# A fused adaLN spectral and MLP layer, forward and backward: sums of x, small rows, index tables, one modulation row and two w1 loads stand elsewhere in the order

## The chip, the core and the metric

The kernel runs on one core of a Trainium2 chip. The metric is the device time of one execution in microseconds (us). The profile is of one execution. Its span runs from the first to the last instruction, and the execution's own time is a little longer than that.

## What is computed

Forward, with x of 2048 tokens by 1024 features:

```python
mod = silu(c) @ w_mod                      # six rows of 1024: sa, ca, ga, sb, cb, gb
h = layernorm(x) * (1 + ca) + sa
x = x + ga * irfft2(rfft2(h) * (w_r + 1j * w_i))
h = layernorm(x) * (1 + cb) + sb
y = layernorm(h); z = y @ w1 + b1          # 1024 -> 3584
out = x + gb * (gelu(z) @ w2 + b2)
```

Given grad_out, the kernel returns the output and the gradients with respect to x, w_r, w_i, w1, b1, w2, b2, c and w_mod. All of it is in bf16 with sums in fp32.

## The kernel before

The work runs as one program of five engines with queues of their own: TensorE (PE) multiplies, VectorE (DVE) and ScalarE (ACT) copy, scale and sum, GpSimd (POOL) makes index tables and issues gathers and stores, SyncE (SP) issues most loads. A scheduler places each engine's instructions; `tc.issue_after(x)` and `ordered()` hold an instruction behind another in that order, `tc.high_priority()` prefers it. Each queue is worked in order: an instruction that waits holds those behind it.

SBUF is cut into regions named by tags (px0 to px5, uv0 to uv3, ph, fr, sma and so on). A new tile on a tag waits until all users of the tile before it are done.

The program's first stage, on which the change bears, has these parts:

- **Modulation rows.** `mod_block(r, h)` (L273 to L284) multiplies half a row of w_mod, a 1 MB block `wblk` that SP loads (L271) into px3, px4 or px5 in turn. Rows: 5 is gb, 1 is ca, 0 is sa, 2, 3 and 4 are ga, sb and cb.
- **Turns of grad_out.** `turn_go(j, cch)` (L541 to L554) turns block j of 512 tokens of grad_out (`go`) with 32 small matmuls into `gBoT[j]`; even pieces are copied out of PSUM by DVE (L550), odd ones by ACT (L553). Block j + 1 is turned between the matmuls of block j.
- **ph = gBoT times w2^T.** For each of 28 pieces fc of the hidden features, `ph_part` (L533) makes four PSUM tiles `pp` of 8 matmuls each. `ph_out` (L523) copies each into a slot `phs[fc % 4]` (three in `pho`, the fourth, `phr`, on tag ph) and POOL stores the slot to `d_ph` when its four tiles are there. The weights `wt` are w2^T in four slots, each loaded by a transposing DMA on SP (`load_w2t`, L342) four pieces ahead. Pieces 0 and 1 are done inside the turns; pieces 2 to 10 (`PH_EARLY` = 10) stand before the spectral part, the rest among its steps and behind it.
- **Sums of x.** x lies in four tiles `x4s[i]`, half of whose rows come by SP and the other half by gathers of POOL. `ln_act` (L455) takes the mean and variance of tile 1 on ACT, with eight passes over 128x1024; `ln_dve` (L470) those of tiles 0, 2 and 3 on DVE; `norm_act` (L496) normalises on ACT.
- **Index tables.** The sine and cosine matrices come from tables of integers: POOL multiplies (L378), DVE masks (L405), ACT takes the sine (L410). `gidx` on tag px0 holds two tables; so the third waits until ACT has read the first. Six tables of 128x1024 make the token matrices `smA` and `smB`, four of 128x512 make `em`.
- **Folds.** L927 to L938: DVE multiplies the normalised tiles in `fbuf` by 1 + ca and folds them along tokens and features, and adds the folded row of sa (`saf`). The spectral part's first matmuls (`pu`, L613) read the folded tiles. They stand in PE's queue behind piece 10 of ph.
- **Small rows.** `small_rows` (L900) makes grad b2's row by one small matmul (`ptr`, L210), stores it from `gb2r` to out_7, and turns b1 into a column (L205). The space for these rows is the end of `genv`, the scratch of the index tables on tag px2. The spectral part's weights `ws2` come next on px2, partly by SP and partly by gathers of POOL (L633).

The spectral part then alternates matmuls with DVE's complex products over eight pairs. `consume_fwd` (L943) works through its four results while PE does the rest of ph. After that come the MLP forward (`z_block` L1036, `bo_pass` L1089), with w1 in seven tiles of 1 MB loaded on SP by `load_w1` (L977), and the backward products. `load_w1` is called in the loop over fc (L991) with one tile at fc = 24, one at 25 and five at 27; the first two lie on px2 and px0.

## Time and profile before

| what | us |
|---|---|
| three runs | 1400.81, 1403.65, 1410.85 |
| the profiled execution, its own time | 1399.52 |
| its span | 1397.7 |
| PE busy in the span | 1360.1 |
| PE idle in the first 140.5 us | 26.2 |
| PE idle from there to 400 us | 6.9 |
| DVE busy in the span | 1069.4 |

Read from the windows by stage: PE is busy 97% of the span. It does the same matmuls whatever their order, so the time goes where PE waits, and where its clock is low behind a wait. In a row of the timeline, the first number is the start, the second the time from the start of the first to the end of the last of the instructions that the row merges, and the bracket gives the engine's idle time before it and what ended that.

### The profile page before, as it was taken

Reading aid. Unit: us, or ns where it says so; the run is one execution under the profiler, and the core shown is the slowest. Engines: PE = TensorE matmul, PEld = TensorE weight load, DVE = VectorE, ACT = ScalarE, POOL = GpSimd, SP = SyncE. Lnnn points to the kernel's source line nnn. Section 1 sums busy time; section 2 is a strip of 40 time slices with the busy share of each in tenths; the row PEclk is TensorE's granted clock in tenths of the full one; section 3 lists DMA queues with packets and bytes.
Section 4 is the critical chain, followed back from the end, with each engine's and each line's share of the span. In section 5 each row is a group of like instructions: output and inputs, shape, how many; then the busy total and the mean of one; then the engine's idle time right before and its main releaser. Section 6 shows DMA issues by size and latency. Waiting matters only on the chain.

```text
span 1397.7 us, 18662 instructions
## 1 busy us (share of the span) xinstructions
PE 1360.1 (97%) x6931; PEld 655.8 (47%) x6931; DVE 1069.4 (77%) x1479; ACT 763.4 (55%) x1082; POOL 380.0 (27%) x438
## 2 busy tenths in 40 slices
PE   6898999998999999999999999999999999999999
PEld 3343657443344444444444444444555555454444
DVE  5787698998899787787721297889987678968990
ACT  4762756675887765665602765436633364544311
POOL 4266271220212122122121010111444320332341
PEclk9999999999999999999999999999999999999999
DMA  9964474799888687597899869988679969899991
GB/s 325 296 192 121 128 181 144 219 268 350 239 252 270 220 268 256 176 281 241 235 324 252 202 197 247 330 264 220 209 237 265 239 143 250 216 246 251 293 333 66
DMA packets 356177, 330.08 MB, mean 236 GB/s; under 512 B 203834, under 2 KB 298448, under 8 KB 355958
## 3 DMA queue, kind: packets, MB, share of 16 engines
q1 hardware_dynamic: 313990, 200.76, 55.6%
q0 software_dynamic: 35328, 120.26, 25.2%
q10 hardware_dynamic: 6768, 7.87, 1.7%
q8 instruction: 54, 0.88, 0.3%
q14 instruction: 37, 0.30, 0.1%
HBM read 165.73 MB, written 114.87 MB: 201 GB/s over the span
## 4 chain that ended last, share of the span: by engine, by line
PE 74%; DVE 4%; ACT 3%; DMA 2%; issue 1%; DVEq 0%; ACTq 0%
PE pg L1205 14%; PE gw2acc L1377 14%; PE gw1acc L1641 14%; PE pbo L1105 11%; PE pz L1051 9%; PE pp L537 6%; DVE gt L195 2%; PE po L845 2%; DMA wt<-in_B_w_dram 1%; PE pcs L652 1%; PE pu L1521 1%; DMA w2sA<-in_B_w_dram 1%; ACT gt L1062 1%; ACT gt L1054 1%; ACT gt L1064 1%
## 5 line engine op out<-in xcount | busy, mean ns | idle before, releaser
L537 PE MATMUL pp<-gBoT,wt 128*128 128x512 bf16 x832 | 190.2, 386 | 9.7 <-ACT pho L529 4.8
L1205 PE MATMUL pg<-w1T,gzr 128*128 128x512 bf16 x896 | 196.0, 379 | 0.0
L1641 PE MATMUL gw1acc<-gzh,n3n 128*128 128x512 bf16 x640 | 139.6, 379 | 0.0
L1051 PEld LDWEIGHTS <-w 128*128 128x128 bf16 x896 | 87.7, 98 | 110.3 <-issue 7.2
L1205 PEld LDWEIGHTS <-gzr 128*128 128x128 bf16 x896 | 86.6, 98 | 108.6 <-issue 6.1
L1641 PEld LDWEIGHTS <-n3n 128*128 128x128 bf16 x896 | 87.4, 98 | 105.2 <-issue 1.3
L537 PEld LDWEIGHTS <-wt 128*128 128x128 bf16 x832 | 82.3, 99 | 108.2 <-issue 14.6
L1051 PE MATMUL pz<-n3Ta,w 128*128 128x512 bf16 x448 | 100.5, 384 | 2.6 <-ACT gt L1054 2.6
L1051 PE MATMUL pz<-n3Tb,w 128*128 128x512 bf16 x448 | 99.2, 379 | 0.2 <-DVE w2sD L1127 0.2
L195 DVE TENSOR_TENSOR ct<-ct 128x2048 bf16<-128x2048 bf16 (+1 forms) x84 | 91.4, 1116 | 2.3 <-ACT ct L1334 1.4
L1105 PEld LDWEIGHTS <-hhA 128*128 128x128 bf16 x608 | 58.9, 98 | 72.6 <-issue 2.3
L1645 ACT CAST gwo<-gw1acc 128x512 bf16<-128x512 f32 x56 | 32.4, 583 | 110.4 <-PE gw1acc L1641 93.5
L1054 ACT ACTIVATE gt<-pz,b_col 128x512 bf16<-128x512 f32 x112 | 72.2, 684 | 37.2 <-PE pz L1051 37.0
L1377 PE MATMUL gw2acc<-gB,hhsA 128*128 128x512 bf16 x416 | 92.4, 379 | 0.0
L1062 ACT ACTIVATE gt<-gt 128x2048 bf16<-128x2048 bf16 x28 | 53.5, 1911 | 56.3 <-DVE gt L195 56.3
L195 DVE TENSOR_TENSOR gt<-gt,gt 128x2048 bf16<-128x2048 bf16 x56 | 68.3, 1223 | 14.7 <-ACT gt L1064 13.5
L1385 ACT CAST gwo<-gw2acc 128x512 bf16<-128x512 f32 x40 | 23.6, 589 | 87.4 <-PE gw2acc L1377 70.2
L1377 PEld LDWEIGHTS <-hhsA 128*128 128x128 bf16 x416 | 40.8, 98 | 47.1
L529 ACT CAST pho<-pp 128x512 bf16<-128x512 f32 x55 | 31.1, 585 | 49.3 <-PE pp L537 39.3
L1058 ACT ACTIVATE gt<-gt 128x2048 bf16<-128x2048 bf16 x28 | 53.4, 1907 | 5.1 <-DVE w2sA L195 2.3
L1641 PE MATMUL gw1acc<-gzu,n3n 128*128 128x512 bf16 x256 | 55.4, 379 | 0.0
L1064 ACT ACTIVATE gt<-gt 128x2048 bf16<-128x2048 bf16 x28 | 53.4, 1909 | 0.5
(385 smaller groups left out, 2593.9 us busy)
## 6 DMA issues: line engine op xcount, KB each, us to landing
gzr<-d_gz SPq DMA_DIRECT2D x28, 512.0 KB
wblk<-in_w_mod_dram SPq DMA_DIRECT2D x12, 1024.0 KB
d_ph<-pho POOLq DMA_DIRECT2D x21, 512.0 KB
out_dram<-otl POOLq DMA_DIRECT2D x40, 256.0 KB
d_hh<-hhA POOLq DMA_DIRECT2D x19, 512.0 KB
wrw<-in_w_mod_dram SPq DMA_DIRECT2D x32, 256.0 KB
out_dram<-gwo POOLq DMA_DIRECT2D x57, 128.0 KB
w<-in_B_w_dram SPq DMA_DIRECT2D x7, 1024.0 KB
```

Of the source, the lines that this page charges most:

```text
L195: return nc.vector.tensor_tensor(out=out, in0=a, in1=b, op=op)
L537: last_pe[0] = nc.tensor.matmul(pp[:], lhsT=wt[:, fc % 4, cch, :], rhs=gBoT[j][:, cch, :], start=(cch == 0), stop=(cch == NDC - 1))
L1051: last_pe[0] = nc.tensor.matmul(pz[:], lhsT=w1s[g][:, cch, k * P:(k + 1) * P], rhs=n3T[:, cch, :], start=(cch == 0), stop=(cch == NDC - 1))
L1054: z_in = nc.scalar.activation(out=zb[:, k, :], in_=pz[:], func=ACT.Identity, bias=b1_col[:, fc:fc + 1], scale=1.0)
L1058: nc.scalar.activation(out=av, in_=zb, func=ACT.Square)
L1062: nc.scalar.activation(out=sg, in_=bv, func=ACT.Sigmoid, scale=2.0 * GK)
L1064: nc.scalar.activation(out=bv, in_=bv, func=ACT.Sigmoid, scale=-2.0 * GK)
L1105: last_pe[0] = nc.tensor.matmul(pbs[i][:], lhsT=hh[:, k, i * P:(i + 1) * P], rhs=wp[:, k, :], start=False, stop=(g == 6 and k == 3))
L1205: last_pg[0] = nc.tensor.matmul(pgs[i][:], lhsT=gzs[b, g][:, k, i * P:(i + 1) * P], rhs=w1Ts[g][:, k, h * KH:(h + 1) * KH], start=(g == 0 ...
L1377: nc.tensor.matmul(acc[:], lhsT=hh_of(fc)[:, t, :], rhs=gBs[t // 4][:, t % 4, h * KH:(h + 1) * KH], start=(t == 0), stop=(t == NT - 1))
L1641: nc.tensor.matmul(acc[:], lhsT=n3ns[t // 4][:, t % 4, cch * P:(cch + 1) * P], rhs=gz2[t // 8][:, t % 8, :], start=(t == 0), stop=(t == NT ...
L1645: w1g["ev"] = nc.scalar.copy(out=ob, in_=acc[:])
```

## The change

- The small rows (c, grad b2, b1) lie in a tile `phx` on tag ph, beside the reversing matrix `irev`, no longer in `genv`. `small_rows` is called at fc = 2, not 4, and the fourth slot `phr` (also on tag ph) is opened behind it.
- The sums of x tiles 0 and 1, and their norms, are ordered behind the last copies of grad_out's second turn (`turn_in`), no longer ahead of the turns.
- Two more index tables, `gidx2` on tag px1 (where grad_out's block 0 lay), make four; tables 2 and 3 are made right behind the first turn. `em1`, also on px1, is opened behind the token tables.
- The blocks of row 0 (sa) stand behind piece 3 of ph. `PH_EARLY` is 9, and the blocks of rows 2 to 4 follow pieces 5 and 7.
- The loads of x tiles 2 and 3 are issued behind the earlier POOL work, in `load_x_turned`.
- The first two tiles of w1 are loaded at fc = 14, in the spectral part.
- A copy of `pa` in the MLP stage (block b = 0) is on ACT, no longer on DVE.

```diff
-    irev = reg.tile([P, P], BF16, name="irev", tag="ph")[:]
+    phx = reg.tile([P, 4 * P], BF16, name="phx", tag="ph")
+    irev = phx[:, 0:P]
...
-    genv = reg.tile([P, 3136 + 3 * P], BF16, name="genv", tag="px2")
-    c8, gb2r, b1r = (genv[0:n, 3136 + k * P:3136 + (k + 1) * P] for k, n in enumerate((NDC, NDC, NFC)))
+    genv = reg.tile([P, 3136], BF16, name="genv", tag="px2")
+    c8, gb2r, b1r = (phx[0:n, (k + 1) * P:(k + 2) * P] for k, n in enumerate((NDC, NDC, NFC)))
...
+    gslots = [gidx[:, 0, :], gidx[:, 1, :]]
...
-        idx = gidx[:, gcount[0] % 2, :]
+        idx = gslots[gcount[0]] if gcount[0] < 4 else gslots[gcount[0] % 2]
...
-    ln_act(x4s[1], 0, 1, fbuf[:, 1])
-    with tc.issue_after(u_in.ins):
-        ln_dve(x4s[0], 0, 0)
-    x_sqrt = sqrt_in[0]
-    for i in range(2):
-        norm_act(fbuf[:, i], x4s[i], 0, i)
...
     for cch in range(NDC):
         turn_go(0, cch)
+    gidx2 = reg.tile([P, 2, 1024], I32, name="gidx2", tag="px1")
+    gslots += [gidx2[:, 0, :], gidx2[:, 1, :]]
+    first_idx += [token_idx(k) for k in (2, 3)]
...
+        if j == 0:
+            with tc.issue_after(turn_in[1].ins):
+                ln_act(x4s[1], 0, 1, fbuf[:, 1])
+            with tc.issue_after(turn_in[0].ins):
+                ln_dve(x4s[0], 0, 0)
+            x_sqrt = sqrt_in[0]
+            for i in range(2):
+                norm_act(fbuf[:, i], x4s[i], 0, i)
...
-    gen_mats()
     for i in (2, 3):
-        load_tok(x4s[i], A_x, i)
+        load_x_plain(i)
+        load_x_turned(i)
+    em1 = gen_mats()
...
-    for h in range(2):
-        wm[0, h] = mod_tile()
-        mod_load(0, h, wm[0, h][:], nc.sync)
-        with ordered():
-            mod_block(0, h, wm[0, h][:])
-    nc.vector.tensor_scalar(out=sar[:, 0], in0=sar[:, 0], scalar1=8.0, scalar2=None, op0=ALU.mult)
-    fold_d(saf.rearrange("p (c d) -> p c d", c=1), sar[:, 0], sar[:, 1])
-    phs.append(reg.tile([P, 4, BW], BF16, name="phr", tag="ph")[:])
...
-    PH_EARLY = 10
+    PH_EARLY = 9
...
-        if fc == 4:
+        if fc == 2:
             with ordered():
                 small_rows()
-        if fc in (3, 5):
-            with tc.issue_after(last_pe[0].ins):
-                for r, h in late_mods[3 * (fc // 2 - 1):3 * (fc // 2)]:
+            phs.append(reg.tile([P, 4, BW], BF16, name="phr", tag="ph")[:])
+        if fc == 3:
+            for h in range(2):
+                with ordered():
+                    mod_block(0, h)
+            nc.vector.tensor_scalar(out=sar[:, 0], in0=sar[:, 0], scalar1=8.0, scalar2=None, op0=ALU.mult)
+            fold_d(saf.rearrange("p (c d) -> p c d", c=1), sar[:, 0], sar[:, 1])
+        if fc in (5, 7):
+            with ordered():
+                for r, h in late_mods[3 * (fc // 2 - 2):3 * (fc // 2 - 1)]:
                     mod_block(r, h)
...
-            load_w1({24: 1, 25: 1, 27: 5}.get(fc, 0))
+            load_w1({14: 2, 27: 5}.get(fc, 0))
...
-                nc.vector.tensor_copy(out=gacc[:, cs_], in_=pa[:])
+                nc.scalar.copy(out=gacc[:, cs_], in_=pa[:])
```

What this makes of the queues is seen in three places. First ACT, between grad_out's first turn (gBoT_133) and its fourth (gBoT_136); `fbuf,sv<-x_1` is one of the eight passes over x. Before:

```order
L553 ACTIVATE gBoT_133,gu<-pt,gb_col 128x512 x4
L458 ACTIVATE fbuf,sv<-x_1_139 128x1024
L553 ACTIVATE gBoT_134,gu<-pt,gb_col 128x512
L458 ACTIVATE fbuf,sv<-x_1_139 128x1024
L553 ACTIVATE gBoT_134,gu<-pt,gb_col 128x512 x2
L529 CAST pho<-pp 128x4x128
L553 ACTIVATE gBoT_134,gu<-pt,gb_col 128x512
L458 ACTIVATE fbuf,sv<-x_1_139 128x1024 x2
```

And now:

```order
L551 ACTIVATE gBoT_133,gu<-pt,gb_col 128x512 x4
L551 ACTIVATE gBoT_134,gu<-pt,gb_col 128x512
L525 CAST pho<-pp 128x4x128
L551 ACTIVATE gBoT_134,gu<-pt,gb_col 128x512 x3
L525 CAST pho<-pp 128x4x128
L460 ACTIVATE fbuf,sv<-x_1_139 128x1024
L551 ACTIVATE gBoT_135,gu<-pt,gb_col 128x512
L460 ACTIVATE fbuf,sv<-x_1_139 128x1024
```

The four copies of the second turn (gBoT_134) have no pass over x ahead of them any more; the passes stand among those of the third and fourth.

Second POOL, from the last index tables (`gidx`) to the stores of ph; `ws` are the gathers of the spectral weights, `out_dram` the store of grad b2's row. Before:

```order
L378 TENSOR_SCALAR gidx<-genv 128x256 x2
L590 TENSOR_SCALAR em_555<-em_555 128x2
L591 TENSOR_SCALAR em_555<-em_555 128x2
L592 DMA d_E<-em_555 128x4096
L531 DMA d_ph<-pho 128x2048
L906 DMA out_dram<-genv 8x128
L633 DMA ws_1191<-in_A_w_r_dram,xu 128x513
L633 DMA ws_1191<-in_A_w_i_dram,xu 128x513
L633 DMA ws_1191<-in_A_w_r_dram,xu 128x513
L633 DMA ws_1191<-in_A_w_i_dram,xu 128x513
L531 DMA d_ph<-pho 128x2048 x2
L531 DMA d_ph<-phr 128x2048
```

And now:

```order
L527 DMA d_ph<-phr 128x2048
L379 TENSOR_SCALAR gidx<-genv 128x256 x6
L642 DMA ws_1150<-in_A_w_r_dram,xu 128x513
L642 DMA ws_1150<-in_A_w_i_dram,xu 128x513
L642 DMA ws_1150<-in_A_w_r_dram,xu 128x513
L642 DMA ws_1150<-in_A_w_i_dram,xu 128x513
L598 TENSOR_SCALAR em_582<-em_582 128x2
L599 TENSOR_SCALAR em_582<-em_582 128x2
L600 DMA d_E<-em_582 128x4096
L527 DMA d_ph<-pho 128x2048 x3
```

The gathers follow the last table directly, ahead of `em` and of three stores of ph; the store of grad b2's row has moved up, between the stores of pieces 2 and 3.

Third SP, behind the spectral weights' last pair: w2^T (`wt`) and w1 (`w_0`, `w_1` and so on). Before:

```order
L342 DMA_TRANSPOSE wt<-in_B_w_dram 128x8x128 x9
L982 DMA w_0_3000<-in_B_w_dram 128x8x512
L342 DMA_TRANSPOSE wt<-in_B_w_dram 128x8x128
L982 DMA w_1_3029<-in_B_w_dram 128x8x512
L342 DMA_TRANSPOSE wt<-in_B_w_dram 128x8x128 x2
L982 DMA w_2_3079<-in_B_w_dram 128x8x512
```

And now:

```order
L343 DMA_TRANSPOSE wt<-in_B_w_dram 128x8x128
L988 DMA w_1_2546<-in_B_w_dram 128x8x512
L988 DMA w_0_2544<-in_B_w_dram 128x8x512
L343 DMA_TRANSPOSE wt<-in_B_w_dram 128x8x128 x12
L988 DMA w_2_3080<-in_B_w_dram 128x8x512
```

The two loads of w1 stand ahead of the last twelve blocks of w2^T, no longer between them.

On PE, the first matmul of the spectral part has 320 matmuls of ph ahead of it where it had 352, and between the last matmul of the spectral part and the first turn of n3 stand 265 where there were 232. From there on the order of PE's stages is as it was.

More of the change, by code (lines that the diff above doesn't have):

```diff
@@ L539, in ph_part @@
             ph_out(fc, j, pp)
+    turn_in = [None, None]
     def turn_go(j, cch):
```

9 lines of the change are left out of this document (5 added, 4 removed).

## The prediction

> **What bounds the kernel now.** I read the windows by stage first, then TensorE's waits, then its timeline at each of them.
>
> ```profile
> core 0: us, PE busy (x) PEld busy (x) DVE busy (x) ACT busy (x) POOL busy (x), PEclk, DMA share, GB/s
> 0.00:140.50 140.50, 114.31 (x588) 53.18 (x589) 103.99 (x184) 75.77 (x123) 73.58 (x80) 0.95 0.77 232
> 140.50:240.00 99.50, 98.73 (x683) 66.38 (x682) 81.76 (x107) 66.65 (x115) 39.78 (x32) 1.00 0.56 153
> 240.00:400.00 160.00, 153.83 (x723) 69.62 (x721) 145.38 (x208) 114.12 (x146) 30.42 (x36) 0.98 0.88 263
> 400.00:741.00 341.00, 340.06 (x1604) 151.44 (x1603) 253.96 (x319) 205.81 (x190) 69.74 (x77) 1.00 0.82 253
> ```
>
> TensorE is the bound: it is busy all but 0.8 of 99.5 us in the spectral part and all but 0.9 of 341 us in the MLP. What can be won lies in two stages, 26.2 us of idle time before 140.5 and 6.2 between 240 and 400; they are also the two whose granted clock is below 1.00. Who ends those waits:
>
> ```profile
> PE pm L279 <- DMA wblk<-in_w_mod_dram: 9.5, 3, 5.4
> PE pp L537 <- ACT pho L529: 4.8, 2, 4.3
> PE pt L546 <- ACT gBoT L553: 4.0, 4, 2.2
> PE pp L537 <- DMA wt<-in_B_w_dram: 3.6, 1, 3.6
> PE pp L537 <- DVE pho L529: 1.4, 1, 1.4
> PE pt L546 <- DVE gBoT L550: 1.1, 2, 0.7
> PE pz L1051 <- DVE w2sD L1127: 0.2, 1, 0.2
> ```
>
> Three of them are long, and behind each the matmuls run slower for a while:
>
> ```profile
> 56.26 3.60 PE L279 MATMUL pm<-wblk,u_b 128*128 128x512 bf16 x8 [5.41 <-DMA wblk<-in_w_mod_dram]
> 72.13 5.34 PE L279 MATMUL pm<-wblk,u_b 128*128 128x512 bf16 x24
> 98.78 27.79 PE L537 MATMUL pp<-gBoT,wt 128*128 128x512 bf16 x128
> 130.84 9.79 PE L537 MATMUL pp<-gBoT,wt 128*128 128x512 bf16 x32 [4.27 <-ACT pho L529]
> 140.48 1.04 PE L613 MATMUL pu<-smA,fbuf 128*128 128x256 bf16 x8
> 319.39 8.77 PE L537 MATMUL pp<-gBoT,wt 128*128 128x512 bf16 x32 [3.56 <-DMA wt<-in_B_w_dram]
> ```
>
> At full clock a matmul takes 27.79/128 = 0.217 us, so a piece of ph (32 of them) takes 6.95 us, and 8 of a modulation block 5.34/3 = 1.78. The slow clock added 3.60 - 1.78 = 1.8 us, 9.79 - 6.95 = 2.8 and 8.77 - 6.95 = 1.8.
>
> **The change, part by part: TensorE.** The sa row's second block was issued with three others and landed only when TensorE had stood for 5.41 us.
>
> ```profile
> 46.45 13.80 SPq L271 DMA_DIRECT2D wblk<-in_w_mod_dram  x4
> ```
>
> Its load keeps its place on SP, but its matmuls now stand behind pieces 2 and 3 of ph, 13.9 us of work: 5.4 + 1.8, and 0.2 at the block before it, are won (7.4). Without that cover the 5.4 would be back.
>
> The 4.27 us at 126.6 are a chain over four engines. POOL stood in one gather of ws, four stores of ph waited behind it, their slots were not free, and ACT's copy, then TensorE, waited:
>
> ```profile
> 78.12 3.91 POOL L378 TENSOR_SCALAR gidx<-genv 128x256 int32<-128x256 f32 x2
> 92.44 0.55 POOL L906 DMA_DIRECT2D out_dram<-genv  x1
> 95.79 25.66 POOL L633 DMA_INDIRECT ws<-in_A_w_r_dram,xu  x1 [2.80 <-PE pm L279]
> 126.29 1.17 POOL L531 DMA_DIRECT2D d_ph<-pho  x2
> 130.21 2.05 ACT L529 CAST pho<-pp 128x512 bf16<-128x512 f32 x4 [9.92 <-DMA d_ph<-pho]
> ```
>
> With the small rows out of px2 the gathers no longer wait for the store of grad b2's row and start right behind the last table. POOL had that done at 78.1 + 3.9 = 82.0, 13.8 us ahead of the gathers, and this end moves forward with the rest, to near 74 (by the 7.8 us found below), where DVE still has copies out of PSUM between its folds. I take the chain as gone: 4.27 + 2.8 = 7.1; it is a rival below.
>
> The copies of the second turn stood behind passes over x that themselves waited for x:
>
> ```profile
> 23.19 1.06 ACT L458 ACTIVATE fbuf<-x 128x1024 bf16<-128x1024 bf16 x1 [5.44 <-DMA x<-in_A_x_dram,xu]
> 25.06 0.27 PE L546 MATMUL pt<-ident,go 128*128 128x128 bf16 x2 [2.24 <-ACT gBoT L553]
> ```
>
> At most 4.0 + 1.1 are won, at least nothing, since grad_out's next block may be what is late next: the first stage moves data nearly all the time (DMA share 0.77 over all of it). I take half, 2.5. In it is a cost: DVE's mask of the third table now stands ahead of the second turn's copies and waits until POOL may write where grad_out's block 0 lay; I put it between 0 and 1 us. The 1.4 us behind DVE's copies I leave as they are: such copies still stand between folds. Issuing x's last gathers later costs nothing while they land before DVE's sums of tiles 2 and 3, which stand behind those of tile 0.
>
> One piece of ph moves from ahead of the spectral part to behind it: 6.95 us earlier there, 6.95 later afterwards, neutral for TensorE's sum. So TensorE would be ready for its first spectral matmul at 140.48 - 6.95 - 7.4 - 7.1 - 2.5 = **116.5**.
>
> **But DVE must have folded x by then.** Its last fold ends at 130.30 + 0.69 = 131.0, and so far TensorE came 9.5 us after it. Now it would come 14.5 us before. How much earlier can DVE be?
>
> ```profile
> 14.50:54.80 40.30, 29.24 (x214) 15.94 (x213) 34.03 (x87) 32.95 (x62) 7.74 (x10) 1.00 1.10 327
> 54.80:62.00 7.20, 5.74 (x16) 2.10 (x17) 0.03 (x1) 2.11 (x3) 0.00 (x0) 0.55 1.03 347
> 62.00:131.10 69.10, 62.93 (x291) 28.29 (x290) 64.93 (x86) 35.13 (x50) 52.64 (x30) 0.99 0.55 155
> 61.97 0.69 DVE L529 CAST pho<-pp 128x512 bf16<-128x512 f32 x1 [7.18 <-PE pp L537]
> 130.30 0.69 DVE L195 TENSOR_TENSOR fbuf<-fbuf,sb_saf 128x1024 bf16<-128x1024 bf16 x1
> L195 DVE TENSOR_TENSOR fbuf<-fbuf,rows 128x4096 bf16<-128x4096 bf16 x4 | 9.1, 2278 | 0.0
> L405 DVE TENSOR_SCALAR gidx<-gidx 128x1024 int32<-128x1024 int32 x3 | 2.5, 819 | 1.1 <-POOL gidx L378 1.1
> L405 DVE TENSOR_SCALAR gidx<-gidx 128x512 int32<-128x512 int32 x4 | 1.7, 427 | 3.0 <-POOL gidx L378 3.0
> ```
>
> (The third column of numbers behind the stretch is DVE.) DVE has 99.0 us of work between 14.5 and 131.1 and stands idle for 17.6: 6.3 early, 7.2 in the wait that the late sa block caused, 4.1 later, all of it for index tables. The change takes none of the work away. It takes the 7.2 away, and with two tables made early some of the 4.1; I take 0.6, as three of the four us belong to the small tables, which still pass through two slots. The early idle stays, for the sums of x now start later. So the folds end at 131.0 - 7.2 - 0.6 = **123.2**; the bounds are 131.0 (a new wait for the old one) and 131.0 - 17.6 = 113.4 (no idle time).
>
> TensorE then waits 6.7 us, which brings the slow clock: 1.8 to 2.8 by the three rows, I take 2.3. The spectral part starts, in effect, at 125.5 instead of 140.48: 15.0 won, less the 6.95 that come back: **8.0**. (The same from the other side: 17.0 us of stalls and slow clock go, 9.0 of a new one come.)
>
> **w1.** Two loads of 1 MB stood between the last blocks of w2^T on SP:
>
> ```profile
> 288.43 1.45 SPq L982 DMA_DIRECT2D w<-in_B_w_dram  x1
> 293.58 8.50 SPq L342 DMA_TRANSPOSE wt<-in_B_w_dram  x1
> 302.13 0.57 SPq L982 DMA_DIRECT2D w<-in_B_w_dram  x1
> 302.80 9.55 SPq L342 DMA_TRANSPOSE wt<-in_B_w_dram  x2
> 239.80 50.07 PE pp L537 x232
> 209.98 1.30 DVE L195 TENSOR_TENSOR qa<-qa,qb 128x1026 bf16<-128x1026 bf16 x2
> ```
>
> The block of w2^T issued at 302.80 was waited for until 319.39. Now both loads go out when the eight pairs are done with px2 and px0, near 210 on the old clock, where the DMA share is 0.56. Behind them on SP stand twelve blocks of w2^T, the first of which TensorE needs only once the spectral part is over (239.8 before), so 30 us cover the 2 MB. The gain is 3.56 + 1.8 = 5.4 at most and 0 if other traffic makes the block late; I take **5.0**, since the row shows the block right behind a w1 load. The copy moved to ACT is worth the 0.2 us by which TensorE waited for it: **0.2**.
>
> **Sum:** 8.0 + 5.0 + 0.2 = 13.2 us. The profiled execution took 1399.52 (span 1397.7), and would take 1386.3; it lies 4.1 below the median of the three runs, 1403.65, against which the forecast is 1390.4, so **1390 us**.
>
> **A page against the trace.** The Trainium skill, "SBUF — State Buffer", section "SBUF: two separate sides", says that GpSimd and VectorE share a port pair under an exclusive lock: the loser "fully blocks" until the other's instruction is over, and descriptors of a GpSimd DMA starve under VectorE's two-port modes. The gather of 25.66 us agrees in kind, but not in length: VectorE's longest instruction in that time took 2.28 us, so the lock must have been lost again and again. By the page's rule a gather would wait for one instruction, the first rival below would have no weight, and the sum would be the one above; by the row that rival stands, with its 1397.
>
> **Rivals.**
>
> 1. *The gathers are held again.* They start behind the last table, and if none gets through before DVE's unbroken run of folds, they stand until its next small operations (before, the first gather ended within 1 us of them). That run ends 7.8 us earlier now, so the ph stores are free at 126.3 - 7.8 = 118.5 and land 3.9 later (126.29 to 130.21), at 122.4. TensorE then does piece 9 with the slow clock, until 132.2: 8.3 - 6.95 + 5.2 = 6.5 won, **1397**. For it: the four gathers still stand ahead of the stores. Against: one piece fewer is waiting, and DVE copies out of PSUM when they start.
> 2. *DVE is quicker.* If the sums of x fill its early idle time as well, TensorE never waits and starts at 116.5 to 118: 24.0 - 6.95 + 5.2 = 22.2 won, **1381**. Against: the sums now wait for the second turn.
> 3. *DVE's 7.2 us turn into another wait*, for the norms on ACT, say, whose sums end later: folds at 131.0, start at 133.3, 7.2 - 6.95 + 5.2 = 5.4 won, **1398**; with the wait for w2^T unchanged too, 1403.
> 4. *Slower: the fourth slot of ph.* Piece 3's copies now need the space that the store of grad b2's row reads. That store can be issued only behind DVE's sums of x tile 3. DVE was all but through with them at 54.8 and now has two masks (0.82 each) and a copy (0.69) more ahead, so the store goes out near 57.1. Before, the next user of its space started 3.4 us after its issue (92.44 to 95.79), so it lands near 60.5, and TensorE wants the copies at 116.5 less six pieces and six blocks (52.4), at 64.1. ACT stands at such a copy too, with the remaining sines behind it, and so the folds. A landing 13 us later, near 74, uses the gain up; the longest landing above, 16.6 us (302.80 to 319.39), would give 73.7, folds at 136.4 and a second slow clock of 2.3, so 2.3 us lost and **1406**. Against: 2 KB at a time of free queues took 3.4.
>
> **How the numbers follow.** Chances: the forecast 0.50 (its own range 1384 to 1396), rival 1 0.05, rival 2 0.18, rival 3 0.19, rival 4 0.08. The range of 8 in 10 reaches from rival 2, less the 4 us by which runs differ, to rival 3 with w2^T still late: 1377 to 1403. A measurement here tells about 1% from no change, 14 us, so the line is at 1389.6: rival 2 and half of the forecast lie below it, 0.44; of rival 4 I put 0.05 past 1% on the other side, since an ACT queue that stands there holds every later copy too; 0.51 is left within.
>
> **What would show it.** Right: no wait for wblk at the sa row; no ph copy that waits for a store near 120; the gathers of ws issued near 74; the last fold near 123, and TensorE waiting some 6 us for it ahead of its first spectral matmul; no wait for wt near 300. Wrong: TensorE waiting elsewhere before 125, a fold ending past 131, or a gather of over 20 us.

## The result, and the profile after

Five executions of the changed kernel took 1385.27 to 1394.34 us, median 1392.09, beside 1403.65 for the kernel before: a ratio of 0.990, 95% interval 0.986 to 0.994 (forecast 1390, range 1377 to 1403). The profiled execution took 1385.27, 14.25 less than the one before; the sum of the prediction was 13.2. In a later group the same program had a median of 1386.76 (six executions; ratio 0.9896, 0.9865 to 0.9928). All ratios here are of undisturbed executions, and need not equal the quotient of two medians.

The windows by stage of the kernel after (columns as before):

```profile
0.00:140.50 140.50, 120.03 (x672) 61.24 (x673) 112.05 (x198) 86.74 (x140) 47.28 (x80) 0.98 0.81 235
140.50:240.00 99.50, 98.73 (x644) 62.66 (x643) 88.12 (x114) 67.44 (x116) 43.70 (x36) 1.00 0.63 186
240.00:400.00 160.00, 156.07 (x748) 71.35 (x747) 144.24 (x199) 118.10 (x144) 31.89 (x37) 1.00 0.87 267
```

TensorE's idle time in the first stretch fell from 26.2 to 20.5 us, and the spectral part now begins well inside it; POOL's busy time there fell from 73.58 to 47.28, nearly all of it the gather that no longer stands. Who ends TensorE's waits now, in the kernel after:

```profile
PE pu L622 <- DVE fbuf L196: 5.5, 1, 5.5
PE pz L1057 <- ACT gt L1060: 3.9, 3, 2.3
PE pm L280 <- DMA wblk<-in_w_mod_dram: 3.9, 1, 3.9
PE pt L544 <- DMA go<-in_grad_out_dram: 2.9, 2, 2.7
PE pt L544 <- ACT gBoT L551: 2.2, 1, 2.2
...
PE pp L533 <- DVE pho L525: 1.8, 1, 1.8
...
PE pp L533 <- ACT pho L525: 1.1, 1, 1.1
```

The three long waits of before are not in it: the 3.9 us for `wblk` is the wait for the first blocks of w_mod at 6.23, which the kernel before has too, and `wt` is missing altogether. At the top stands the wait that the prediction put there, for the last fold. (`...` marks lines left out, here and below.) TensorE's timeline of the kernel after at these places:

```profile
59.10 3.62 PE L280 MATMUL pm<-wblk,u_b 128*128 128x512 bf16 x16
...
117.68 0.27 PE L622 MATMUL pu<-smA,fbuf 128*128 128x256 bf16 x1
123.41 1.68 PE L622 MATMUL pu<-smA,fbuf 128*128 128x256 bf16 x7 [5.46 <-DVE fbuf L196]
...
305.88 7.07 PE L533 MATMUL pp<-gBoT,wt 128*128 128x512 bf16 x32
```

Both sa blocks run without a gap, and the last piece of ph runs without one at 305.88. And DVE's timeline, at the fourth slot of ph and at the last fold:

```profile
61.91 1.29 DVE L525 CAST phr<-pp 128x512 bf16<-128x512 f32 x2 [2.45 <-DMA out_dram<-phx]
...
122.66 0.69 DVE L196 TENSOR_TENSOR fbuf<-fbuf,sb_saf 128x1024 bf16<-128x1024 bf16 x1
```

The last fold ends at 122.66 + 0.69 = 123.35 (forecast 123.2). POOL's four gathers in the kernel after:

```profile
71.88 1.10 POOL L642 DMA_INDIRECT ws<-in_A_w_r_dram,xu  x1 [0.28 <-POOL gidx L379]
73.28 1.44 POOL L642 DMA_INDIRECT ws<-in_A_w_i_dram,xu  x1 [0.30 <-issue]
75.02 0.95 POOL L642 DMA_INDIRECT ws<-in_A_w_r_dram,xu  x1 [0.31 <-issue]
76.28 1.64 POOL L642 DMA_INDIRECT ws<-in_A_w_i_dram,xu  x1 [0.30 <-issue]
```

They go out near 72 (forecast 74) in 1 to 1.6 us each, where the first took 25.66 us.

Followed through the program, the lead of the profile after over the one before is 16.3 us at the first spectral matmul on `smB` (154.07 to 137.76), 9.8 at the first turn of n3 (289.71 to 279.92), since the moved piece has come back there, 15.2 at the first `pz` (327.99 to 312.79), since the wait for w2^T is gone, 15.4 at the second half of z, and 14.3 at the end, where waits of about a microsecond differ. From the second profiles of the two kernels the lead at `smB` is 14.5 (152.78 to 138.25).

### The profile page after: what moved, and what is told of

It is laid out like the page before. It is cut to its first block, busy times and chain, and to the rows that moved or that the text cites. A ratio compares the mean times of both kernels' runs of the same rounds, so it can differ in the third digit from the quotient of the medians.

```text
span 1383.5 us, 18662 instructions
## 1 busy us (share of the span) xinstructions
PE 1352.7 (98%) x6931; PEld 654.8 (47%) x6931; DVE 1066.7 (77%) x1474; ACT 766.3 (55%) x1087; POOL 357.3 (26%) x438
## 4 chain that ended last, share of the span: by engine, by line
PE 76%; DVE 13%; ACT 4%; DMA 4%; issue 2%; SPq 1%; POOL 1%; DVEq 0%; ACTq 0%; POOLq 0%
PE pg L1211 14%; PE gw1acc L1647 14%; PE gw2acc L1383 13%; PE pbo L1111 13%; PE pz L1057 12%; DVE ct L196 4%; DVE fbuf L196 2%; DVE st L477 2%; DMA x<-in_A_x_dram 2%; DVE x L196 1%; PE pcs L661 1%; PE po L854 1%; PE pu L622 1%; PE pv L732 1%; PE pu L615 1%
## 5 line engine op out<-in xcount | busy, mean ns | idle before, releaser
L533 PE MATMUL pp<-gBoT,wt 128*128 128x512 bf16 x832 | 185.0, 379 | 2.9 <-DVE pho L525 1.8
L1383 PE MATMUL gw2acc<-gB,otl 128*128 128x512 bf16 x224 | 50.0, 379 | 0.0
```

The source lines that it names most:

```text
L533: last_pe[0] = nc.tensor.matmul(pp[:], lhsT=wt[:, fc % 4, cch, :], rhs=gBoT[j][:, cch, :], start=(cch == 0), stop=(cch == NDC - 1))
L1383: nc.tensor.matmul(acc[:], lhsT=hh_of(fc)[:, t, :], rhs=gBs[t // 4][:, t % 4, h * KH:(h + 1) * KH], start=(t == 0), stop=(t == NT - 1))
```

## The experiments

Each kernel is the kernel before with one part of the change, or the changed kernel with one part undone. "smB" is the start of the first spectral matmul on `smB`, "pz" that of the first `pz`, both from the one profile. With ten early pieces instead of nine, smB is 6.95 later for the same state of things. The median of the kernel before in the four groups was 1403.7, 1404.1, 1401.0 and 1401.4.

| kernel | smB | pz | span | median (executions) | ratio to before, 95% |
|---|---|---|---|---|---|
| before | 154.07 | 327.99 | 1397.7 | 1403.65 (5) | |
| before_again | 152.78 | 330.93 | 1408.1 | 1402.97 (10) | 1.0006, 0.9972 to 1.0040 |
| w1_alone | 152.90 | 321.32 | 1393.8 | 1398.87 (10) | 0.9971, 0.9942 to 0.9999 |
| rows_alone | 149.19 | 326.36 | 1403.5 | 1397.25 (10) | 0.9972, 0.9937 to 1.0008 |
| sa_alone | 143.38 | 311.84 | 1386.2 | 1390.28 (10) | 0.9921, 0.9887 to 0.9956 |
| piece9_alone | 146.76 | 323.25 | 1399.4 | 1399.84 (10) | 0.9985, 0.9966 to 1.0004 |
| changed | 137.76 | 312.79 | 1383.5 | 1392.09 (5) | 0.9900, 0.9857 to 0.9942 |
| changed_again | 138.25 | 313.30 | 1386.7 | 1386.76 (6) | 0.9896, 0.9865 to 0.9928 |
| w1_late | 139.87 | 314.90 | 1386.6 | 1387.11 (6) | 0.9890, 0.9863 to 0.9918 |
| sa_ahead | 141.09 | 317.60 | 1389.5 | 1396.53 (10) | 0.9960, 0.9932 to 0.9988 |
| sums_ahead | 141.78 | 317.44 | 1393.3 | 1395.10 (10) | 0.9954, 0.9930 to 0.9979 |
| rows_px2 | 137.97 | 313.02 | 1387.3 | 1386.45 (4) | 0.9876, 0.9836 to 0.9915 |
| gb2_apart | 135.64 | 312.25 | 1388.3 | 1387.55 (4) | 0.9884, 0.9843 to 0.9925 |
| piece10 | 137.93 | 306.39 | 1383.3 | 1385.24 (6) | 0.9865, 0.9834 to 0.9897 |

### Two controls

No edit in either. For the kernel before:

> The kernel before once more, nothing edited: which of its waits come back? If they are set by the program's order, TensorE again waits 5.4 us for the sa row's second block, 4.3 us for ACT's copy behind the held gather and 3.6 us for the last block of w2^T, smB within 1 us of 154.07 and the first pz within 1 us of 328. If a wait is a race between transfers, its length differs by microseconds from the first profile: from the kernel with the sa row alone and the changed kernel with the late w1 loads, whose order at that place is the same and which did not wait, I expect this of the wait for w2^T (0 to 6 us), and of the wait for the sa block, since all kernels that have that block ahead of piece 2 spread over 13 us or more and most of the others over 4 to 8.

For the changed kernel:

> The changed kernel once more, nothing edited, as a measure of how far executions of one program differ and as the partner of the three kernels below on the same chip. Its profiled execution (1385.27) was the fastest of five (median 1392.09); the version with ten early pieces gave 1385.24 as a median of six. If the waits of the first stage are set by the program's order, TensorE again stands 5 to 6 us ahead of its second spectral matmul and smB starts within 1 us of 137.8; what differs between executions then lies behind 300 us, at waits for transfers and for ACT. Median 1387 to 1393.

Measured: the waits of the first stage belong to the program, to a microsecond or two. In the kernel before, the sa wait was 5.41 us again and the gather took 25.64 (25.66). The copy behind it cost TensorE 2.62 (4.27), with 2.3 us waited at earlier copies where it had been 1.9; so smB came 1.3 us earlier, just outside what was expected, and every gain at smB below that is counted from 154.07 is 1.3 smaller when counted from this profile. In the changed kernel TensorE's wait for the folds was 5.45 (5.46). What differs more from execution to execution lies behind 300 us: the wait for w2^T was 7.58 where it had been 3.56, and at one place near 880 to 900 TensorE waited 0, 3.75, 0 and 2.23 us in these four profiles. So the effects below are read at smB and pz, and from the ratios, and not from the difference of two spans.

### The sa row: alone, and undone

`sa_alone`, on the kernel before, with the fold of sa behind the two blocks:

```diff
-    for h in range(2):
-        wm[0, h] = mod_tile()
-        mod_load(0, h, wm[0, h][:], nc.sync)
-        with ordered():
-            mod_block(0, h, wm[0, h][:])
...
+        if fc == 2:
+            for h in range(2):
+                with ordered():
+                    mod_block(0, h)
```

> The kernel before with only the two sa blocks moved, here behind piece 2 of ph (fc = 2), since behind piece 3 stand the late rows in this kernel. Theory: piece 2 (6.95 us) covers the load, the wait of 5.41 us and its 1.8 us of slow clock go, DVE's wait of 7.18 us too, and the folds end near 124; the gather stays held until DVE's unbroken folds are over, which end about 7 us earlier, so TensorE's wait for ph's store stays near 4 us: first spectral matmul near 133.3, span near 1390.5. Rival: the wait moves on (another block of w_mod or of w2^T is late instead), and the first spectral matmul stays later than 137: span 1394 or more.

`sa_ahead`, on the changed kernel, puts the two blocks and the fold of sa ahead of the loop over fc again:

```diff
+    for h in range(2):
+        with ordered():
+            mod_block(0, h)
...
-        if fc == 3:
-            for h in range(2):
-                with ordered():
-                    mod_block(0, h)
```

> The changed kernel with the two sa blocks back ahead of piece 2 of ph. Theory (the prediction's step on the sa row): TensorE stands 5 us for the second block with 1.8 us of slow clock, DVE stands near 7 us too (it has nothing but copies of the stalled pieces), the last fold ends near 130 instead of 123.35, TensorE waits 5 us there as well, smB near 144.5 (137.76), 6 to 7 us more in all: the median near 1398. Rival (the two waits overlap: DVE has the sums of x, masks and folds to do meanwhile, and only TensorE loses): fold end within 1.5 us of 123.35, TensorE's wait there shrinks from 5.46 to near 0, smB near 138, the median within 2 us of the changed kernel's.

TensorE's timeline of the kernel with the sa row moved alone:

```profile
56.55 1.90 PE L279 MATMUL pm<-wblk,u_b 128*128 128x512 bf16 x8 [1.33 <-DMA wblk<-in_w_mod_dram]
...
80.64 8.62 PE L537 MATMUL pp<-gBoT,wt 128*128 128x512 bf16 x32 [2.23 <-ACT pho L529]
...
122.89 7.07 PE L537 MATMUL pp<-gBoT,wt 128*128 128x512 bf16 x32 [0.83 <-ACT pho L529]
```

The 5.41 us became 1.33. Part of the gain is lost at a copy wait at 80.64, 2.23 us with some 1.6 of slow clock behind it; at the same copies the kernel before waited 1.37 and 0.53 in its first profile, and 2.32 in its second, there with the slow clock too (32 matmuls in 8.75 us). The gather's chain, still there (its first gather took 23.92 us), now costs only 0.83 us in place of 4.27: the gather's end followed the end of DVE's folds, 7 us earlier, and TensorE arrived only 4.5 us earlier. The last fold ended at 122.98 + 0.69 = 123.7 (expected near 124). So smB gained 10.7 (9.4 from the second profile of the kernel before) where 7.2 was expected. The theory held, and it missed that the chain shrinks with it. This part alone gives as much at smB as the whole change: 143.38 with ten early pieces, where the changed kernel would have 137.76 + 6.95 = 144.71, and pz starts at 311.84, where it has 312.79 (here no wait for w2^T came, of which more below). Its ratio, 0.9921, is a little higher than 0.9900 and 0.9896, but the intervals overlap: that the other parts add to it is not shown.

Undone in the changed kernel, it falls between theory and rival. TensorE's timeline of that kernel:

```profile
48.32 3.49 PE L280 MATMUL pm<-wblk,u_b 128*128 128x512 bf16 x8 [4.95 <-DMA wblk<-in_w_mod_dram]
56.30 1.90 PE L280 MATMUL pm<-wblk,u_b 128*128 128x512 bf16 x8 [2.33 <-DMA wblk<-in_w_mod_dram]
73.99 13.97 PE L533 MATMUL pp<-gBoT,wt 128*128 128x512 bf16 x64 [3.77 <-ACT phr L525]
...
128.02 0.94 PE L622 MATMUL pu<-smA,fbuf 128*128 128x256 bf16 x7 [1.96 <-DVE fbuf L196]
```

The waits at the blocks come back, 7.3 us, and the wait for the folds shrinks from 5.46 to 1.96; the folds end at 127.96, 4.6 later, not 7. DVE waited 5.4 us for the two blocks, but no longer 2.45 for the store to out_7; the row at 73.99 is TensorE's wait for ACT's copies into the fourth slot, which stood 1.72 us for that store. So smB moved 3 us and pz 4 to 5. The times say more: 1396.53, with a ratio 0.0064 higher, about 9 us. The profiled execution (1391.37) was the second fastest of ten, and what the slower ones lose I did not see; that stays open.

### The small rows and the held gather: alone, and undone

`rows_alone`, on the kernel before, with the rows in `phx` on tag ph:

```diff
-    genv = reg.tile([P, 3136 + 3 * P], BF16, name="genv", tag="px2")
+    genv = reg.tile([P, 3136], BF16, name="genv", tag="px2")
...
-        if fc == 4:
+        if fc == 2:
             with ordered():
                 small_rows()
+            phs.append(reg.tile([P, 4, BW], BF16, name="phr", tag="ph")[:])
```

> The kernel before with only the small rows out of px2 (in phx on tag ph, small_rows at fc = 2, phr opened behind it). Theory: the chain over POOL's gather is what held ph's stores, so the four gathers go out behind the last table (near 82) while DVE still has copies out of PSUM, each takes 1 to 2 us, ACT's copy no longer waits 9.9 us for a store, and TensorE's 4.27 us at 126.57 and 2.8 us of slow clock go. The folds end near 131 and TensorE needs them at 133.4, so the whole 7.1 us comes through: first spectral matmul near 133.5, span near 1390.6. Rival 1 of the prediction: DVE's folds have begun when the gathers start, and a gather stands over 15 us again; TensorE waits as before, 140.5, span 1397. Rival: the store that now holds phr's copies puts DVE and ACT 2 to 3 us back as in the changed kernel, folds at 133 to 134: span 1391 to 1393.

`rows_px2` is the changed kernel with these lines the other way round, and `phr` opened at fc = 2.

> The changed kernel with the small rows back in px2 and behind piece 4 (as before), the fourth slot phr opened ahead of piece 3 without them. Two effects: the gathers of ws wait for the store of grad b2's row and go out near 86 instead of 71.9, and DVE and ACT no longer wait 2.45 and 2.85 us for that store ahead of piece 3's copies. Theory: the first gather stands 15 us or more, since DVE's two-input products run without a break by then; the stores of pieces 5 to 7 stand behind it, TensorE waits for copies ahead of piece 9, 2 to 6 us; but the folds end near 121 and TensorE's own wait for them (5.46) takes most of that up: smB 135.5 to 141, the median within 4 us of the changed kernel's. Rival (the whole price of the chain comes through even here): smB at 144 or later, the median 1398 or more. Rival (no chain: at that place the gathers run in 1 to 2 us each): gathers under 5 us, smB near 135.3, the median 2 us lower.

Alone, the gathers took 1.10 to 1.89 us from 80.81 on, no ph store was held, and smB came 4.9 us earlier (3.6 from the second profile of the kernel before), not 7.1: one of the late blocks of w_mod was now waited for, 1.48 us, and the small matmul `ptr` 0.99. The interval of the ratio holds 1, so no gain in time is shown. Rival 1 of the prediction, and the rival of a late fold, did not show.

Undone in the changed kernel, the chain returned whole. POOL's timeline of that kernel, then TensorE's:

```profile
82.53 1.04 POOL L642 DMA_INDIRECT ws<-in_A_w_r_dram,xu  x1 [4.93 <-issue]
...
85.36 27.42 POOL L642 DMA_INDIRECT ws<-in_A_w_r_dram,xu  x1 [0.30 <-issue]
```

```profile
119.17 0.38 PE L533 MATMUL pp<-gBoT,wt 128*128 128x512 bf16 x1 [2.96 <-ACT pho L525]
122.46 1.46 PE L622 MATMUL pu<-smA,fbuf 128*128 128x256 bf16 x6 [2.91 <-DVE fbuf L196]
```

The gather that began as DVE's copies ended stood 27.42 us; the one 3 us earlier took 1.04. TensorE waited 2.96 us for the copy behind it, and then only 2.91 for the folds: 5.87 together, where the changed kernel has 5.46. smB is 137.97, and the time is the same within the intervals. The theory held: what the chain costs is hidden in the wait for the folds.

### The sums of x, undone

On the changed kernel, the sums and the norms again ahead of the turns:

```diff
-        if j == 0:
-            with tc.issue_after(turn_in[1].ins):
-                ln_act(x4s[1], 0, 1, fbuf[:, 1])
...
+    ln_act(x4s[1], 0, 1, fbuf[:, 1])
+    with tc.issue_after(u_in.ins):
+        ln_dve(x4s[0], 0, 0)
```

> The changed kernel with the sums of x and their norms ordered ahead of grad_out's turns again. Theory (the prediction's step on the second turn): the second turn's copies stand behind passes over x that wait for x, TensorE loses 2 to 4 us there, but all of it ahead of 117, where it now waits 5.46 us for the folds, so it costs nothing itself; DVE gets its sums earlier, as early as x lands, and the folds end within 1.5 us of 122 to 123.4: smB 136.5 to 138.5, median within 2 us of the changed kernel's. Rival (the sums of x ahead of the turns delay DVE's and ACT's copies, and through TensorE the modulation rows and the folds): fold end past 125, smB past 140, 2 us or more lost. Rival (DVE's early idle time was the sums waiting for the turn, the prediction's second rival): fold end near 120, 3 us won.

DVE's timeline of that kernel, then TensorE's:

```profile
18.75 0.69 DVE L477 BATCH_NORM_STATS2 st<-x 128x6 f32<-128x512 bf16 x1 [2.61 <-DMA x<-in_A_x_dram,xu]
...
48.13 1.29 DVE L477 BATCH_NORM_STATS2 st<-x 128x6 f32<-128x512 bf16 x2 [5.97 <-DMA x<-in_A_x_dram]
```

```profile
20.16 0.37 PE L550 MATMUL pt<-ident,go 128*128 128x128 bf16 x2 [3.76 <-DVE gBoT L554]
...
62.70 0.27 PE L211 MATMUL ptr<-ident,gb_bf 128*8 128x128 bf16 x1 [3.50 <-DVE gb_bf L901]
```

A sum that waits for x (2.61 us) stands ahead of the copies of the first turn, and TensorE waits 3.76 for them; a later wait of DVE for x, 5.97 us, stands ahead of the copy that the small matmul `ptr` needs. TensorE reaches its first spectral matmul at 126.9 (117.1 to 117.7), the folds end at 126.75 (122.8 and 123.35), smB is 3.5 to 4 later, and the ratio is 0.0058 higher, about 8 us. The first rival is right: this part of the change carries weight, through both engines.

### w1, the last block of w2^T, and the piece

`w1_alone` on the kernel before (`w1_late` is the same line the other way, on the changed kernel):

```diff
-            load_w1({24: 1, 25: 1, 27: 5}.get(fc, 0))
+            load_w1({14: 2, 27: 5}.get(fc, 0))
```

> The kernel before with only the two w1 loads moved to fc = 14. Theory (this step of the prediction alone): the wait of 3.56 us for w2^T at 319.39 and its 1.8 us of slow clock go, nothing else moves: the first spectral matmul stays near 140.5, the first pz starts near 322.6 (327.99 before), span 5.0 to 5.4 lower, near 1392.5 (before 1397.7). Rival: the two loads delay the twelve blocks of w2^T behind them or the spectral weights, and the wait comes back at another block: pz near 328, span 1396 to 1399.

> The changed kernel with the two w1 loads back at fc = 24 and 25. Theory (the prediction's step on w1): TensorE waits for the last block of w2^T again, 3.6 us with 1.8 us of slow clock, first pz near 318 (312.79), the median 4 to 5 us above the changed kernel's. Rival, from the kernel with the sa row alone, where the loads stood at 24 and 25 and no wait was seen: whether that block is late hangs on the other traffic, not on the order alone (the wait was 3.56, 6.29 and 0 in three profiles that all have the old places); then pz near 312.8 in this profile and a median within 2 us of the changed kernel's.

Alone, the wait went: pz came 6.7 earlier, 1.2 of it from smB, and so 5.5 from w1 (theory 5.4). But undone in the changed kernel there was no wait either: pz came 1.6 later than in that kernel's second profile, just as smB did. The step of the prediction had the right price and not the whole reason. In five profiles with the old places the wait was 3.56, 7.58, 6.29 (`rows_alone`), 0 (`sa_alone`) and 0 (`w1_late`). I compared when the last block is issued with when ACT issues its store of 1 MB to `d_n`, and tested it with one more part alone, on the kernel before:

```diff
-    PH_EARLY = 10
+    PH_EARLY = 9
```

> The kernel before with only PH_EARLY = 9: one piece of ph moved behind the spectral part, w1's loads still at fc = 24 and 25. Two questions. First, what the piece is worth by itself: TensorE leaves the early pieces at 126.6 or before, the folds end at 131, ACT's copies of piece 9 are held until 130 behind the gather, so the spectral part starts at 131 plus 1 to 2 us of slow clock, smB near 146 (154.07 and 152.78 before), and the piece comes back behind it: nothing is won or lost at pz by that. Second, why the last block of w2^T is late. My theory: with the old places of the w1 loads that block is issued at the same time as ACT's store of 1 MB to d_n. Where the store is ahead of it by 0.4 to 2.3 us (the kernel before twice, the small rows alone), it lands 10.5 to 13 us after its issue and TensorE waits 3.56 to 7.58; where it is 0.3 us behind (the sa row alone) or 7 us ahead (the changed kernel with late w1 loads), there is no wait. One piece less ahead moves the block about 7 us away from that store, so no wait for wt here: the first pz at 320.5 to 323.5. Rival (the sa row's new place or another part of the change took that wait away): a wait of 3 us or more for wt near 315, and the first pz at 327 to 332.

The kernel before, second profile: SP's last two blocks (one row, the second issued at 309.5), ACT's store, TensorE's wait:

```profile
300.75 17.49 SPq L342 DMA_TRANSPOSE wt<-in_B_w_dram  x2
```

```profile
307.17 0.38 ACTq L967 DMA_DIRECT2D d_n<-n  x1
```

```profile
322.02 9.08 PE L537 MATMUL pp<-gBoT,wt 128*128 128x512 bf16 x31 [7.58 <-DMA wt<-in_B_w_dram]
```

And the kernel with nine early pieces alone: all its blocks of w2^T in one row (the starts of the first and the last are behind the three durations), the store, TensorE's last piece:

```profile
L342 SPq DMA_TRANSPOSE wt<-in_B_w_dram x11: 1232/1238/2159, 238.8 to 309.0; - x11
```

```profile
299.53 0.38 ACTq L967 DMA_DIRECT2D d_n<-n  x1
```

```profile
316.35 7.07 PE L537 MATMUL pp<-gBoT,wt 128*128 128x512 bf16 x32
```

With the store 9.5 us ahead of the block there was no wait; with 2.3 us between them 7.58. pz at 323.25 was inside the interval expected, and smB at 146.76 where 146 was. So with either edit to the kernel before, the early loads of w1 or the moved piece, this wait was gone in the one profile of each. With the sa row alone it was gone too; there the store came 0.3 us behind the block, at 297.81. That the store is the cause fits all these profiles, but it is not shown. With the early loads of w1 alone the store also came 0.3 us behind the block (307.29 and 307.0), so that run does not tell the order of w1's loads from the store. And the moved piece took the block farther from the w1 load ahead of it as well: 13.5 us behind it (295.55 to 309.0), where it was 9.4 in the second profile of the kernel before (300.08 to 309.5). The w1 load alone is not enough for a wait, since with the sa row alone the block stood 7.0 us behind it and nothing waited. What happens inside the queues was not looked at.

### Filling the hole, and DVE's 2.45 us

`piece10`, on the changed kernel, is a candidate that could beat both:

```diff
-    PH_EARLY = 9
+    PH_EARLY = 10
```

> The changed kernel with ten early pieces of ph again (PH_EARLY = 10), all else as it is. Theory: the spectral part starts when DVE's last fold ends (123.35 in the changed kernel) and TensorE stands 5.46 us for it, with about 1.3 us of slow clock behind. A piece of 6.95 us put there fills this hole: TensorE is ready near 124.6, later than the fold, so it does not wait; the first spectral matmul on smB starts near 138 as before (137.76), and the piece is missing behind the spectral part, so the first pz starts near 306 (312.79 now) and the end comes 5 to 7 us earlier: a span near 1377.5, where the changed kernel's profile had 1383.5. Rival (the hole is not what sets the spectral part's time; the products on DVE or the weights' loads do): the piece goes in front, the products end as late as now, smB near 144.7, pz near 312.8, span 1383 to 1385.

`gb2_apart`, on the changed kernel (grad b2's row alone back in px2's tile):

```diff
-    genv = reg.tile([P, 3136], BF16, name="genv", tag="px2")
-    c8, gb2r, b1r = (phx[0:n, (k + 1) * P:(k + 2) * P] for k, n in enumerate((NDC, NDC, NFC)))
+    genv = reg.tile([P, 3136 + P], BF16, name="genv", tag="px2")
+    c8, gb2r, b1r = (phx[0:n, (k + 1) * P:(k + 2) * P] for k, n in enumerate((NDC, NDC, NFC))); gb2r = genv[0:NDC, 3136:3136 + P]
```

> The changed kernel with grad b2's row in px2's tile and only c and b1 beside irev, so that the fourth slot of ph no longer waits for the store to out_7 (the prediction's fourth rival, which showed as a wait of 2.45 us of DVE and 2.85 us of ACT). Theory: DVE's wait goes, the folds are all that TensorE waits for ahead of the spectral part, they end 2.45 us earlier, near 120.5 to 120.9, TensorE waits near 3 us instead of 5.46, smB near 135.5, the end up to 2.4 us earlier. The gathers still go out near 72, since the store lands near 62. Rival (another chain, POOL's tables or ACT's sines, is as late as that store): DVE waits for index tables instead, the folds end past 122, smB within 0.7 us of 138.

Up to smB both theories held. With the tenth piece TensorE does not wait for the folds at all, smB is 137.93, and pz comes 6.4 earlier than in the changed kernel. With the row apart, DVE's 2.45 us are gone, the last fold ends at 120.66, and smB comes 2.1 to 2.6 earlier; TensorE still waits 4.88, for it is ready earlier too, at 115.6. But of these 2 us only 0.5 to 1.0 are left at pz, and the medians are 1385.24 and 1387.55, beside 1386.76 and 1392.09 for the changed kernel. The ratio with ten pieces is 0.003 lower, some 4 us, and the intervals overlap: neither is shown to beat it. The span with ten pieces, 1383.3, is the rival's number and not the theory's 1377.5, though not for the rival's reason: in the profiles a lead goes back behind 340 us. TensorE's timeline of the kernel with ten pieces, then ACT's:

```profile
344.93 8.63 PE L1057 MATMUL pz<-n3Ta,w 128*128 128x512 bf16 x32 [3.15 <-ACT gt L1060]
...
880.22 11.34 PE L1211 MATMUL pg<-w1T,gzr 128*128 128x512 bf16 x44 [3.47 <-ACT gn3a L1227]
```

```profile
870.72 4.63 ACT L502 ACTIVATE n2u<-n2u,stats 128x1024 bf16<-128x1024 bf16 x4 [18.89 <-DMA n2u<-d_x]
```

ACT stood 18.89 us for a load, and the copies that TensorE needed were queued behind its work on that load; in the changed kernel's first profile the load came at 864.89, and ACT then waited for DVE, so that it reached these copies at the same time, 879.39 (879.41 with ten pieces). TensorE came to them 4 us later there (its matmuls on `au`, just ahead, start at 878.25 and 874.30), and did not wait. So the lead of TensorE was lost at work that had not become earlier with it. TensorE in the kernel with the row apart:

```profile
436.95 3.57 PE L1057 MATMUL pz<-n3Tb,w 128*128 128x512 bf16 x8 [4.06 <-ACT w2sD L1133]
```

That is the copy of `pa` which the change moved to ACT; neither profile of the changed kernel has a wait there of over 0.6 us, but four of its variants have one: 4.06 in `gb2_apart`, `sa_ahead` and `sums_ahead`, 2.42 in `rows_px2`. With the copy on DVE (`piece9_alone`) a wait of 3.50 stood at the same place. What makes this wait is not shown; `sa_ahead` and `sums_ahead`, which have it too, reach pz later than the changed kernel, so an earlier arrival is not needed for it.

## Why the prediction came out right, step by step

**TensorE's stalls.** The sa wait went (no gap at 59.10), and so did the chain over POOL (7.1). The sa row was worth somewhat more than the 7.4 of the sum: the row of ph behind its block was slow as well (54 matmuls in 12.64 us at 59.65, which take 11.8 at full clock). The waits of the turns fell from 8.2 to 5.7 us in the lists of waits, the 2.5 that I took. But the long copy wait did not vanish, it moved from the second turn to the third, behind a pass over x that waited 2.56 us for x, and behind it the granted clock was 0.56 from 30.38 to 34.23: 1.7 us that the prediction did not count, so the turns gave some 0.8. (In the second profile the longest wait there was 1.92 us, for grad_out, and no slow clock followed.) The copies of ph, which I left as they were, cost 2.9 us instead of 1.9. With these errors both ways TensorE was ready at 117.7, forecast 116.5.

**The folds.** 123.35, forecast 123.2, by two errors that cancel, which is luck. DVE's idle time from 14.5 up to the last fold fell from 17.6 to 12.2 us, 5.4 and not the 7.8 that I took, since the fourth slot's 2.45 us came in: rival 4 was there in mechanism (store issued at 57.2, landed near 61.9, forecast 57.1 and 60.5), far short of its break-even. (One row was misread in rival 4: the 16.6 us from 302.80 to 319.39 are not one landing, for the row at 302.80 merges two blocks and the second, which TensorE waited for, was issued at 308.9, so 10.5 us. The 1406 hangs on it, the break-even does not.) And DVE had 96.7 us of work in that time, not 99.0. The change does leave the work as it was (183 instructions up to the last fold in both kernels, 102.2 and 101.8 us), but 1.9 us more of it now lies ahead of 14.5, where the prediction began to count: the copies of the first turn begin at 12.92 and not at 14.63. The view that shows it, DVE's column in the windows of the kernel after:

```profile
14.50:54.80 40.30, 35.10 (x231) 18.43 (x231) 32.31 (x83) 32.78 (x61) 11.82 (x15) 0.96 1.09 305
54.80:62.00 7.20, 7.20 (x35) 3.31 (x34) 4.75 (x12) 4.35 (x6) 3.39 (x4) 1.00 1.08 368
62.00:123.40 61.40, 53.04 (x245) 23.69 (x243) 59.63 (x75) 33.31 (x48) 19.65 (x22) 0.99 0.77 221
```

**The new wait.** 5.46 us instead of 6.7. The slow clock behind it cost some 1.3: from the first long `pu` to smB took 14.35 us where it was 13.59, with one matmul of 0.13 done ahead and with one matmul of ph in between where there were three, 0.43 less work. In the second profile, behind a wait of 5.45, the same stretch took 15.39, so 2.4 were lost; the 2.3 that I took lies between the two. The windows of this stretch in the first profile and in the second (the granted clock is the third number from the end):

```profile
123.41:137.76 14.35, 14.06 (x104) 10.71 (x105) 7.51 (x10) 9.90 (x17) 0.00 (x0) 0.91 0.05 11
```

```profile
122.86:138.25 15.39, 15.11 (x105) 11.36 (x105) 7.50 (x10) 10.09 (x17) 0.00 (x0) 0.83 0.05 12
```

The spectral part gained 16.3 for the 15.0 forecast (14.5 from the second profiles), 9.4 after the piece for 8.0.

**w1.** 5.4 us between the turn of n3 and pz, forecast 5.0. Here a reason failed: I wrote that the gain comes from the order on SP. In `w1_late` the changed kernel did without the move of w1. The step that I called neutral, one piece moved behind the spectral part, was enough for the wait to go. Nor is that step neutral for TensorE's sum once TensorE has to wait for the folds: with the piece ahead (`piece10`) it fills that wait, and pz comes 6.4 us earlier.

**The gates.** The prediction's point that what counts is the later of TensorE and DVE is what the undone parts show. The small rows cost nothing when undone: what they save TensorE is hidden in the wait for the folds, and the store that they bring ahead of the fourth slot costs DVE 2.45 us. The sa row and the sums hang on both engines, and undoing either costs 3 to 4 us at smB and 8 to 9 in the times, of which the part behind pz was not found. The parts do not add up: the sa row alone gives as much at smB as all of them. Not tried by themselves were the two further index tables, the later loads of x tiles 2 and 3, the new places of rows 2 to 4 and the copy of `gacc` (0.2).

**What was not in it.** Behind 300 us I carried every microsecond to the end. In the profile after that was nearly so (15.2 at pz, 14.3 at the end), but other profiles lose up to 5 us at one late wait with its slow clock (`piece10`, 3.47 and 11.34 for 44 matmuls of 0.217). `gb2_apart`, 2 us ahead at smB, and `piece10`, 6 us ahead at pz, show some 2 and 4 us of it in their ratios, inside the intervals.

## What to carry to other kernels

Where two engines must both arrive, price a change as the later of the two: undo each part alone in the new kernel, for a part that moves a stage by 5 us alone can be worth nothing there, and one part alone can give as much as all. A wait for a transfer may go for several reasons, and one profile does not tell which; look at what else is issued within a few microseconds of it, and profile the same program twice. Put work that waits for a load behind the copies that another engine needs, not ahead of them.

## What the hardware showed that was not expected

- A GpSimd gather issued just as DVE's long run of two-input bf16 products and sums began stood 23.92 to 27.42 us in all six profiles where that happened (25.64 to 25.66 in four of them); the same gathers took 0.9 to 2.1 us where DVE still had copies out of PSUM or small operations between them. The Trainium skill, "SBUF — State Buffer", section "SBUF: two separate sides", says that the loser of the shared port pair waits for the other's instruction. The longest DVE instruction in those runs took 2.3 us, so the measurement goes beyond that.
- The length of a wait does not tell the slow clock behind it, even in one program at one place. Behind the wait for the folds, 5.46 and 5.45 us, the clock granted up to smB was 0.91 in one profile of the changed kernel and 0.83 in the other. And behind the same wait of 2.28 us near 383, 32 matmuls took 7.07 us in the first, as they do elsewhere, and 8.75 in the second:

```profile
383.25 7.07 PE L1057 MATMUL pz<-n3Ta,w 128*128 128x512 bf16 x32 [2.28 <-ACT gt L1060]
```

```profile
383.77 8.75 PE L1057 MATMUL pz<-n3Ta,w 128*128 128x512 bf16 x32 [2.28 <-ACT gt L1060]
```

- The last block of w2^T, a transposing load behind a 1 MB load on SP, landed 12.5 us after its issue when ACT had issued a 1 MB store 2.3 us ahead of it, and within 7.4 us when the store was 9.5 us ahead and the w1 load 13.5 us ahead instead of 9.4. Which of the two counts is open.
